# Retention attention and a mixer on one core: the order of the weight loads and of the third batch's loads in the first stretch

## The chip, the cores and the metric

The kernel runs on one core of a Trainium2 chip. The metric is the device time of one execution in microseconds (us); it is given as the median of several executions. A profile comes from one further look at a single execution, and its span is a little shorter than the time of that execution.

## The reference, cut to what matters

The inputs are q, k and v of shape (8 batches, 8 heads, 576 positions, 64), all float32, and four weight matrices. Per batch and head the kernel computes decayed causal products without a softmax, puts the heads side by side to a row of 512, and sends the result through a mixer: a low-rank product along the positions (U is 576 x 32, V is 32 x 576), a residual, and a two-layer network with relu (w1 is 512 x 2048, w2 is 2048 x 512).

```python
scores = scale * np.matmul(q, k.transpose(0, 1, 3, 2))
Dmat = np.where(rel >= 0, gamma[:, None, None] ** rel[None, :, :], 0.0)
x = np.matmul(scores * Dmat[None], v)            # then (B, S, H * D)
u = x + (x.transpose(0, 2, 1) @ U @ V).transpose(0, 2, 1)
out = u + np.maximum(u @ w_ch1, 0.0) @ w_ch2
```

## The kernel before

Two batches make a pair of 1152 rows, which is nine chunks of 128 rows; the fifth chunk (index J = 4) holds the last 64 rows of one batch and the first 64 of the next. `order` lists the chunks of all four pairs, so `order[NI]` (NI = 9) is the first chunk of the third batch. All matmuls run in bf16. The attention works chunk by chunk with a running state per head; the decay is put into the rows of q and v (or k) by the scale tables qscale, vscale and vscaleU.

The first pair is handled apart. Its two batches are cut into four units of 256 rows (units 0 and 1 of the first batch, 2 and 3 of the second) and the half chunk J. `load_u` (L625) loads a unit: k, q and v in two halves each, so six transfers of 256 KB, issued by SP. `scale_u` (L656) and `cast_u` (L648) turn them into bf16, mostly on POOL (GpSimd); `T_u` transposes them on PE; `SC_u`, `mask_u`, `RV_u`, `QS_u` and `XS_u` are scores, mask, values, the state's share and the scaling of the result (L773, on DVE); `ST_u` and `Sblk` update the state. `cast_qk` and `prep_v` (L261) do the same casts for the half chunk.

From the third batch on, a chunk is loaded with `load` (L217: k, q and v, 256 KB each, issued by SP at L230), cast by `cast_chunk` (on ACT, DVE and POOL, L280 to L291) and transposed by a DMA, `xbar` (L298, on SP). Then `section` uses it; its scores are L315.

The mixer's first layer is `Y1` (L534, PE, followed by the relu on ACT at L539), one product per block f of 128 columns of w1. The second layer is `Y2` (L568), which runs through all sixteen blocks of w2 for one chunk of 128 rows; its result is added to the residual and stored by POOL (L557, L560).

The weights come by POOL's DMA queue and are cast from float32 to bf16 on the way: `load_w1(f0, f1)` (L196) brings the columns of the blocks f0 to f1, `load_w2(f)` (L200) two blocks of w2. All of w1 comes in six pieces, all of w2 in eight.

The schedule is written out by hand: each engine executes its instructions in the order of the program text, and an instruction that waits holds everything behind it on its engine. `startup` (L884) issues the loads and prepares the first pair; `first_stretch` (L1009) handles the half chunk's second part, units 2 and 3, and fills the gaps with the first layer of the first batch (`y(n)` runs n of its sixteen blocks). After that `merge` interleaves mixer items with the sections of the next batch by cost shares: `ready(n)` casts and transposes chunk NI + n, `fetch(n, which)` loads one. SP thus issues, in this order: the loads of units 0 to 2, of unit 3, of chunks NI to NI + 2 and of k and q of chunk NI + 3, the first transpose, and further loads and transposes in turn.

Two gates hold SP's queue. `load_u` and `load` take an argument `gate`: the engine named there writes one column of the first tile of the load with a memset (L634, L223), and SP's transfer into that tile has to wait for it. In the kernel before, both unit 3 and chunk NI are gated by POOL, so these loads start when POOL comes to the memset in its own order. All staged loads use 15 buffers of one pool in turn, and a load waits until the casts of the buffer's last content are done.

POOL's order in this stretch is: the casts of the half chunk's second part, its values (`prep_v`), the w1 pieces (2, 4) and (4, 6), the scaling of unit 2's k, the casts of its q, w1 (6, 8), the memset for unit 3, the casts of unit 2's v, w1 (8, 12), the casts of unit 3's k and q, w1 (12, 16), the memset for chunk NI, the casts of unit 3's v, and the eight pieces of w2.

Of the kernel before, what the change touches and what calls it, by code (L numbers as in the profile page):

```python
# [34 lines left out]
def kernel(  # L35
# [11 lines left out]
    nc = tc.nc  # L47
# [8 lines left out]
    NF = dff // P  # L56
    NCC = dm // P
    NI = 9
# [135 lines left out]
    def load_w1(f0, f1):  # L194
        w = slice(f0 * P, f1 * P)
        nc.gpsimd.dma_start(  # L196
            out=w1_sb[:, :, w], in_=moe_w_ch1[:, w].rearrange("(c p) f -> p c f", p=P))

    def load_w2(f):
        nc.gpsimd.dma_start(  # L200
            out=w2_sb[:, f:f + 2, :],
            in_=moe_w_ch2[f * P:(f + 2) * P, :].rearrange("(f p) d -> p f d", p=P),
        )
# [10 lines left out]

    ch = {}

    def load(pr, i, which, seg=None, gate=None):  # L217
        c = ch.setdefault((pr, i), {})
        for j in which:
            if ("f", j) not in c:  # L220
                c["f", j] = stage.tile([P, H, D], FP32, tag="stage", name="stage_t")
                if gate is not None:
                    gate.memset(c["f", j][:, 0:1, 0:1], 0.0)  # L223
                    gate = None
            dram = (q, k, v)[j]
            for n_seg, (rows, b, t0) in enumerate(parts(pr, i)):
                if seg is not None and n_seg != seg:
                    continue
                n = rows.stop - rows.start
                nc.sync.dma_start(  # L230
                    out=c["f", j][rows, :, :],
                    in_=dram[b, :, t0:t0 + n, :].rearrange("h s d -> s h d"),
                )
# [27 lines left out]
    def prep_v(pr, i, rows=slice(0, P)):  # L261
        c = ch[pr, i]
        if "v" not in c:
            c["v"] = v_pool.tile([P, H, D], BF16, tag="v", name="vt")
        scale_rows(c["v"][rows], c["f", 2], i, rows, nc.gpsimd)
# [618 lines left out]
    def startup():  # L884
        load_u(0, (1, 0))
        load_v_rows()
        load_u(1, (1, 0))
        load_u(0, (2,))
        load(0, J, (1, 0), seg=0)
        load_u(1, (2,))  # L890
        load(0, J, (2,), seg=0)
        load_u_rows()
        load(0, J, (1, 0, 2), seg=1)
        load_u(2, (1, 0, 2))
        nc.gpsimd.memset(st["x", 0][HI, J, :], 0.0)

        warm(10)
        cast_unit(0)
        T_u(0, 1, nc.vector)
        un[0]["off"] = y1_tile(0)[:, 0:4, :].rearrange(  # L900
            "p (a x) (y i) -> p a (x y) i", x=2, i=P)
        nc.vector.memset(un[0]["off"][HI], 0.0)
        warm(5)
        nc.scalar.activation(out=V_b, in_=V_f, func=AF.Copy)
        T_u(0, 0, nc.scalar)
        make_v()
        warm(5)
        SC_u(0, 0, ps_sc, "psc")
        mask_u(0, 0)
        cast_unit(1)  # L910
        cast_u(0, 2, 0, nc.gpsimd)
        cast_u(0, 2, 1, nc.gpsimd)
        cast_u(1, 2, 0, nc.gpsimd)
        load_w1(0, 2)
        cast_u(1, 2, 1, nc.gpsimd)
        T_u(1, 1, nc.scalar)
        SC_u(0, 1, ps_o, "po")
        mask_u(0, 1)
        SC_off(0, ps_sc, "psc")
        warm(3)  # L920
        T_u(1, 0)
        SC_off(1, ps_o, "po")
        warm(3)
        SC_u(1, 0, ps_sc, "psc")
        mask_u(1, 0)
        cast_qk(0, J, LO, nc.scalar, nc.vector, decay=True)
        SC_u(1, 1, ps_o, "po")
        mask_u(1, 1)

        acc1 = pss_tile()  # L930
        ST_u(0, ALL, acc1, True)
        Sblk(acc1, 1)
        RV_u(0, 0)
        RV_u(0, 1)
        RV_off()
        XS_u(0)
        T_J(LO)
        acc2 = ps_big.tile([P, NHP, P], FP32, tag="big", name="pss2")
        ST_u(0, ALL, acc2, True)
        prep_v(0, J, LO)  # L940
        cast_urows()
        RV_u(1, 0)
        SC_J(LO)
        mask_J(LO)
        ST_u(1, LO, acc1, False)
        Sblk(acc1, 2)
        cast_qk(0, J, HI, nc.gpsimd, nc.gpsimd)
        prep_v(0, J, HI)
        load_w1(2, 4)
        load_w1(4, 6)  # L950
        scale_u(2, 0, nc.gpsimd)
        for hh in range(2):
            cast_u(2, 0, hh, nc.gpsimd)
        load_w1(6, 8)
        load_u(3, (1, 0, 2), nc.gpsimd)
        for hh in range(2):
            cast_u(2, 2, hh, nc.gpsimd)
        load_w1(8, 12)
        scale_u(3, 0, nc.gpsimd)
        for hh in range(2):  # L960
            cast_u(3, 0, hh, nc.gpsimd)
        load_w1(12, 16)
        load(*order[NI], (1, 0, 2), gate=nc.gpsimd)
        for hh in range(2):
            cast_u(3, 2, hh, nc.gpsimd)
        for f in range(0, NF, 2):
            load_w2(f)
        RV_u(1, 1)
        QS_u(1, 0, 1)
        XS_u(1, 0, 1)  # L970
        ST_u(1, ALL, acc2, False)
        Sblk(acc2, 3)
        QS_u(1, 1, 2)
        XS_u(1, 1, 2)
        RV_J(LO)
        QS_J(3)
        XS_J(LO)

        xT = [ps_big.tile([P, dm], FP32, tag="big", name="xT") for _ in range(3)]
        xT.append(ps_sc.tile([P, dm], FP32, tag="psc", name="xT"))  # L980

        def to_xT(lo, hi):
            for i in range(lo, hi):
                for cc in range(NCC):
                    nc.tensor.matmul(
                        xT[cc][:, i * P:(i + 1) * P],
                        st["x", 0][:, i, cc * P:(cc + 1) * P], ident,
                        start=(i == 0), stop=True, skip_group_check=True,
                    )

        to_xT(0, 2)
        MA, _, _, _ = mixer_items(0, 0, split=True)
        MA((ps_o, "po"))
        to_xT(2, J)
        for cc in range(NCC):
            g = slice(cc * R, (cc + 1) * R)
            nc.tensor.matmul(
                xT[cc], st["a", 0][g, :], V4[g, HALF:HALF + 4 * P],
                start=False, stop=True, skip_group_check=True,
            )  # L1000
        for cc in range(NCC):
            o = st["uT", 0][:, :, cc, :]
            i_ = xT[cc].rearrange("p (s t) -> p s t", t=P)
            if cc % 2 == 0:
                nc.scalar.activation(out=o, in_=i_, func=AF.Copy)
            else:
                nc.vector.tensor_copy(out=o, in_=i_)

    def first_stretch():  # L1009

        ys = iter([fn for _, fn in y1_items(0)])

        def y(n):
            for _ in range(n):
                fn = next(ys, None)
                if fn is not None:
                    fn()

        _, MH0, _, outs0 = mixer_items(0, 0, split=True)
        MA1, MH1, MT1, outs1 = mixer_items(0, 1, split=True)  # L1020
        T_J(HI)
        y(1)
        scale_u(2, 1, nc.vector)
        make_u()
        SC_J(HI)
        mask_J(HI)
        y(1)
        acc = pss_tile()
        ST_J(HI, acc)
        Sblk(acc, 0)  # L1030

        def unit(u, slots, last):
            T_u(u, 1, nc.vector)
            if last:
                y(1)
            T_u(u, 0)
            y(1)
            SC_u(u, 0, ps_sc, "psc")
            mask_u(u, 0)
            y(1)  # L1040
            ST_u(u, LO, acc, False)
            Sblk(acc, slots[1])
            SC_u(u, 1, ps_sc, "psc")
            mask_u(u, 1)
            if not last:
                scale_u(3, 1, nc.vector)
            y(1)
            if not last:
                ST_u(u, HI, acc, False)
                Sblk(acc, slots[2])  # L1050
            RV_u(u, 0)
            QS_u(u, 0, slots[0])
            QS_u(u, 1, slots[1])
            if last:
                RV_J(HI)
                XS_J(HI)
            RV_u(u, 1)
            XS_u(u)

        for g in range(NI + 1, NI + 4):  # L1060
            load(*order[g], (1, 0, 2) if g < NI + 3 else (1, 0))
        unit(2, (0, 1, 2), False)
        y(2)
        unit(3, (2, 3), True)
        y(1)
        MA1()
        y(1)
        MH1(outs1[0])
        y(2)
        MT1(outs1[0])  # L1070
        MH1(outs1[1])
        y(16)
        Y1, rest = y1_items(1, by_seg=True)
        Y1(0, 0)
        Y1(1, 0)
        MT1(outs1[1])
        MH0(outs0[0])
        Y1(2, 0)
        for f in range(3):
            Y1(f, 1)  # L1080
        return rest[3:]
# [60 lines left out]
```

## Time and profile before

| what | value |
|---|---|
| five runs | 328.24, 327.23, 330.67, 328.96, 332.22 us; median 328.96 |
| the profiled execution | 328.24 us |
| its span | 326.5 us, granted TensorE clock 1.00 |
| busy: PE, DVE, ACT, POOL | 311.6, 171.5, 143.2, 99.9 us |
| DMA queue of SP | 40.40 MB in 144512 packets |
| DMA queue of POOL | 12.32 MB in 7824 packets |
| w1 pieces issued by POOL at | 16.1, 23.0, 23.8, 27.2, 29.2, 39.4 us |
| w2 pieces issued by POOL at | 42.1 to 47.0 us (the last one's start) |
| unit 3's loads issued by SP | 28.18 to 34.8 us |
| chunk NI's loads issued by SP | from 40.32 us |
| first use of w1's second piece | 29.03 us |
| first use of w2 | 75.8 us |

PE is the matmul engine, DVE the vector engine, ACT the scalar engine, POOL is GpSimd, and SP issues DMAs. Times count from the start of the span. In the page's row of forty slices a digit is the busy share of one slice of 8.16 us in tenths. In an answer of the windows each engine has its busy time and, in brackets, its number of instructions, in the order PE, weight load, DVE, ACT, POOL; then come the granted clock, the mean busy share of the sixteen DMA engines (it can exceed 1, since both queues count) and the GB/s moved. A "landing" is the time from the issue of a DMA to the moment when its data are there.

### The profile page before, as it was taken

What the parts mean: (1) busy time and instruction counts of PE and PEld (TensorE: products, weight loads), DVE (VectorE), ACT (ScalarE), POOL (GpSimd) and SP (SyncE); (2) the same over time, 40 slices, a digit from 0 to 9 for tenths busy, and PEclk for the clock granted to TensorE, in tenths of its full rate; (3) what the DMA queues carried; (4) which work ended last, traced back from release to release, by engine and by line L of the source; (5) the groups of instructions that cost most, each with busy time, mean ns of one, the idle gap of its engine ahead of it and who ended that gap; (6) DMA issues with size and microseconds to landing.
All of it is one profiled execution on the core that took longest, in us unless ns stands there. A gap on an engine that the chain in (4) does not pass through costs nothing.

```text
span 326.5 us, 9076 instructions
## 1 busy us (share of the span) xinstructions
PE 311.6 (95%) x3860; PEld 171.2 (52%) x3885; DVE 171.5 (53%) x336; ACT 143.2 (44%) x326; POOL 99.9 (31%) x169
## 2 busy tenths in 40 slices
PE   8998899979999999999999999999999999999996
PEld 3574455745444444456744444457744444467544
DVE  7666455327745478546754477555744475510012
ACT  3747447874001285038820484048810473047400
POOL 7676470343112724132321414141421500110000
PEclk9999999999999999999999999999999999999999
DMA  7999899999984989979998599969998440340012
GB/s 207 246 228 199 206 196 196 219 208 140 248 189 118 253 179 189 211 172 165 213 156 209 132 174 221 209 152 134 206 197 198 116 68 3 97 114 0 2 73 88
DMA packets 152376, 53.30 MB, mean 163 GB/s; under 512 B 132016, under 2 KB 149808, under 8 KB 152336
## 3 DMA queue, kind: packets, MB, share of 16 engines
q1 hardware_dynamic: 144512, 40.40, 67.2%
q0 software_dynamic: 7824, 12.32, 15.5%
q8 instruction: 30, 0.49, 0.6%
q14 instruction: 10, 0.08, 0.1%
HBM read 36.85 MB, written 9.44 MB: 142 GB/s over the span
## 4 chain that ended last, share of the span: by engine, by line
PE 76%; DMA 8%; SPq 5%; ACT 3%; DVE 2%; issue 2%; POOL 2%; DVEq 0%
PE ps_y L568 36%; PE ps_y L534 32%; DMA qkT<-qk 4%; SPq L636 3%; DMA stage_t<-in_q_dram 3%; PE pp L315 2%; DMA stage_t<-in_v_dram 2%; DVE u L483 2%; SPq L230 1%; PE pp L335 1%; ACT y L539 1%; PE pp L347 1%; PE ps_y L579 1%; PE AB L377 1%; PE pa L450 1%
## 5 line engine op out<-in xcount | busy, mean ns | idle before, releaser
L534 PE MATMUL ps_y<-uT,w_sb 128*128 128x256 bf16 (+2 forms) x768 | 132.9, 326 | 1.8 <-DMA w_sb<-in_moe_w_ch_dram 0.8
L539 ACT ACTIVATE y<-ps_y 128x384 bf16<-128x384 f32 (+2 forms) x192 | 89.7, 491 | 98.7 <-PE ps_y L534 97.6
L568 PE MATMUL ps_y<-w_sb,y 128*128 128x512 bf16 x535 | 123.8, 379 | 2.2 <-issue 1.1
L534 PEld LDWEIGHTS <-w_sb 128*128 128x128 bf16 x768 | 72.2, 98 | 49.3 <-issue 2.5
L568 PEld LDWEIGHTS <-y 128*128 128x128 bf16 x560 | 52.6, 98 | 61.1
L291 POOL TENSOR_TENSOR vt<-stage_t,vscale 64x256 bf16<-64x256 f32 (+1 forms) x81 | 50.1, 619 | 71.2 <-DMA stage_t<-in_v_dram 46.0
L557 DVE TENSOR_TENSOR o_sb<-ps_y,u 128x512 f32<-128x512 f32 (+2 forms) x38 | 25.2, 664 | 81.6 <-PE ps_y L568 79.2
L560 POOL DMA_DIRECT2D out_dram<-o_sb x31 | 17.1, 553 | 104.2 <-DVE o_sb L557 98.4
L323 DVE TENSOR_TENSOR ret<-pp,triH 128x512 bf16<-128x512 f32 x27 | 18.7, 692 | 24.4 <-PE pp L347 19.0
L483 DVE TENSOR_TENSOR u<-ph,xt 128x768 bf16<-128x768 f32 (+2 forms) x24 | 21.8, 951 | 5.9 <-PE ph L477 5.9
L282 DVE CAST qk<-stage_t 64x256 bf16<-64x256 f32 x54 | 19.6, 363 | 6.8 <-DMA stage_t<-in_k_dram 5.6
L456 ACT ACTIVATE a_sb<-pa 128x128 bf16<-128x128 f32 x8 | 2.2, 278 | 43.2 <-PE pa L450 43.2
L363 DVE TENSOR_TENSOR xt<-pp,qscale 128x512 bf16<-128x512 f32 x27 | 18.6, 690 | 4.7 <-PE pp L347 4.2
L402 DVE TENSOR_TENSOR s_sb<-AB,Af 64x256 bf16<-64x256 f32 x42 | 17.7, 422 | 2.1 <-ACT s_sb L397 1.6
L357 DVE COPY q<-qkT 64x256 bf16<-64x256 bf16 x48 | 13.0, 270 | 9.7 <-DMA qkT<-qk 8.7
L283 ACT ACTIVATE qk<-stage_t 128x512 bf16<-128x512 f32 x27 | 16.8, 621 | 0.5 <-DMA stage_t<-in_q_dram 0.5
L395 ACT ACTIVATE Af<-AB 128x256 f32<-128x256 f32 x24 | 9.2, 385 | 8.1 <-PE AB L377 7.6
L654 POOL CAST qk<-stage_t 128x512 bf16<-128x512 f32 x16 | 10.2, 644 | 8.5 <-DMA stage_t<-in_q_dram 4.9
L711 DVE TENSOR_TENSOR ret<-psc,triU 128x1024 bf16<-128x1024 f32 x8 | 9.7, 1221 | 5.5 <-PE psc L703 5.5
L315 PEld LDWEIGHTS <-qkT 64*64 64x64 bf16 x432 | 5.6, 107 | 12.6 <-issue 7.8
L315 PE MATMUL pp<-qkT 64*64 64x64 bf16 x432 | 8.6, 198 | 3.1 <-DMA qkT<-qk 3.1
L280 ACT ACTIVATE qk<-stage_t 128x256 bf16<-128x256 f32 x27 | 11.0, 409 | 0.0
(123 smaller groups left out, 213.3 us busy)
## 6 DMA issues: line engine op xcount, KB each, us to landing
stage_t<-in_k_dram SPq DMA_DIRECT2D x32, 256.0 KB, 4.6
stage_t<-in_q_dram SPq DMA_DIRECT2D x32, 256.0 KB, 5.1
stage_t<-in_v_dram SPq DMA_DIRECT2D x32, 256.0 KB, 5.5
out_dram<-o_sb POOLq DMA_DIRECT2D x31, 256.0 KB, 3.5
w_sb<-in_moe_w_ch_dram POOLq DMA_DIRECT2D x12, 256.0 KB, 8.1
stage_t<-in_k_dram SPq DMA_DIRECT2D x8, 128.0 KB, 3.4
stage_t<-in_q_dram SPq DMA_DIRECT2D x8, 128.0 KB, 3.8
stage_t<-in_v_dram SPq DMA_DIRECT2D x8, 128.0 KB, 5.3
```

The costliest lines, as they stand in the source:

```text
L282: nc.vector.tensor_copy(out=o[to, hl], in_=f[fr, hl])
L291: nc.gpsimd.tensor_tensor(out=o[to, hl], in0=f[fr, hl], in1=w[fr, hl, :, None].to_broadcast([n, NHP, D]), op=ALU.mult)
L315: nc.tensor.matmul(pp[half(m), m ^ hl, hp * D:(hp + 1) * D], qkT[half(hl), NHP + hp, half(m)], qkT[half(hl), hp, half(m ^ hl)], start=True ...
L323: nc.vector.tensor_tensor(out=ret.rearrange("p a b i -> p a (b i)").rearrange("p a (b i) -> p a b i", i=D), in0=pp[:, :, 0:NHP * D].rearra ...
L363: nc.vector.tensor_tensor(out=st["x", pr][:, i, :].rearrange("p (hp hl d) -> p hl hp d", hl=2, d=D), in0=pp[:, :, NHP * D:2 * NHP * D].rea ...
L402: nc.vector.tensor_tensor(out=S_[half(x), 1, :], in0=Bk[half(1 - x)], in1=Af[half(1 - x), now, :], op=ALU.add)
L483: nc.vector.tensor_tensor(out=st["u", par][:, i0 - base:i0 - base + n, w].rearrange("p s (c d) -> p c s d", c=2), in0=ph[k][:, :, 0:n, :], ...
L534: nc.tensor.matmul(ps[:, 0:n, :], w1_sb[:, cc, f * P:(f + 1) * P], st["uT", par][:, c0:c0 + n, cc, :], start=(cc == 0), stop=(cc == NCC - 1),)
L539: nc.scalar.activation(out=st["y1", par][:, f, c0 * P:(c0 + n) * P], in_=ps[:, 0:n, :].rearrange("p s t -> p (s t)"), func=AF.Relu)
L557: nc.vector.tensor_tensor(out=o_sb[:, 0:n], in0=ps[:, 0:n], in1=st["u", par][:, c, w], op=ALU.add)
L560: (nc.sync if last else nc.gpsimd).dma_start(out=out_flat[r0:r0 + P, w], in_=o_sb[:, 0:n])
L568: nc.tensor.matmul(ps, st["y1", par][:, f, c * P:(c + 1) * P], w2_sb[:, f, :], start=(f == 0), stop=(f == NF - 1),)
```

## The change

It has four parts. The gate of `load` is taken out, and chunk NI's loads move from `startup` into the loop of `first_stretch` that already loads the following chunks (g now begins at NI). The eight `load_w2` calls move from the end of `startup` behind unit 3 in `first_stretch`, and a memset on DVE of one column of w2's first block stands in front of them; the first of these loads writes that column too, so POOL waits for DVE there. `load_w1(2, 4)` moves ahead of `prep_v(0, J, HI)`. `load_u(3, ...)` with its gate moves from behind `load_w1(6, 8)` to ahead of the casts of unit 2's q.

```diff
--- before.py
+++ after.py
@@ -214,14 +214,11 @@
 
     ch = {}
 
-    def load(pr, i, which, seg=None, gate=None):
+    def load(pr, i, which, seg=None):
         c = ch.setdefault((pr, i), {})
         for j in which:
             if ("f", j) not in c:
                 c["f", j] = stage.tile([P, H, D], FP32, tag="stage", name="stage_t")
-                if gate is not None:
-                    gate.memset(c["f", j][:, 0:1, 0:1], 0.0)
-                    gate = None
             dram = (q, k, v)[j]
             for n_seg, (rows, b, t0) in enumerate(parts(pr, i)):
                 if seg is not None and n_seg != seg:
@@ -945,14 +942,14 @@
         ST_u(1, LO, acc1, False)
         Sblk(acc1, 2)
         cast_qk(0, J, HI, nc.gpsimd, nc.gpsimd)
+        load_w1(2, 4)
         prep_v(0, J, HI)
-        load_w1(2, 4)
         load_w1(4, 6)
         scale_u(2, 0, nc.gpsimd)
+        load_u(3, (1, 0, 2), nc.gpsimd)
         for hh in range(2):
             cast_u(2, 0, hh, nc.gpsimd)
         load_w1(6, 8)
-        load_u(3, (1, 0, 2), nc.gpsimd)
         for hh in range(2):
             cast_u(2, 2, hh, nc.gpsimd)
         load_w1(8, 12)
@@ -960,11 +957,8 @@
         for hh in range(2):
             cast_u(3, 0, hh, nc.gpsimd)
         load_w1(12, 16)
-        load(*order[NI], (1, 0, 2), gate=nc.gpsimd)
         for hh in range(2):
             cast_u(3, 2, hh, nc.gpsimd)
-        for f in range(0, NF, 2):
-            load_w2(f)
         RV_u(1, 1)
         QS_u(1, 0, 1)
         XS_u(1, 0, 1)
@@ -1057,11 +1051,14 @@
             RV_u(u, 1)
             XS_u(u)
 
-        for g in range(NI + 1, NI + 4):
+        for g in range(NI, NI + 4):
             load(*order[g], (1, 0, 2) if g < NI + 3 else (1, 0))
         unit(2, (0, 1, 2), False)
         y(2)
         unit(3, (2, 3), True)
+        nc.vector.memset(w2_sb[:, 0, 0:1], 0.0)
+        for f in range(0, NF, 2):
+            load_w2(f)
         y(1)
         MA1()
         y(1)
```

## The prediction

> **What bounds the kernel now.** I read the page first, then the waits of PE, then PE's and SP's timelines between 20 and 80 us, then the windows of one microsecond where the DMA row has a hole, and last the landing times of single transfers.
>
> ```profile
> PE 311.6 (95%) x3860; PEld 171.2 (52%) x3885; DVE 171.5 (53%) x336; ACT 143.2 (44%) x326; POOL 99.9 (31%) x169
> PE   8998899979999999999999999999999999999996
> DMA  7999899999984989979998599969998440340012
> ```
>
> PE is busy 95% of the span, so only its idle time can be won. The DMA engines are full from 8 to 90 us but for a dent in the fifth slice (32.6 to 40.8; a slice is 8.16 us): the first stretch is limited by transfers as much as by PE. The waits of PE from 15 to 60 us (first three lines) and from 60 to 100 us (last) say which idle time:
>
> ```profile
> PE pst L674 <- DVE qk L658: 1.0, 1, 1.0
> PE ps_y L534 <- DMA w_sb<-in_moe_w_ch_dram: 0.8, 1, 0.8
> PE pa L450 <- DVE xt L773: 0.5, 1, 0.5
> PE pp L315 <- DMA qkT<-qk: 2.7, 2, 2.4
> ```
>
> The largest is the first scores of the third batch, which wait for the transposed keys. PE's timeline places it (start, length, in brackets the idle time before):
>
> ```profile
> 55.28 12.29 PE L534 MATMUL ps_y<-uT,w_sb 128*128 128x384 bf16 x88
> 69.98 0.32 PE L315 MATMUL pp<-qkT 64*64 64x64 bf16 x16 [2.40 <-DMA qkT<-qk]
> 75.13 0.32 PE L315 MATMUL pp<-qkT 64*64 64x64 bf16 x16 [0.26 <-DMA qkT<-qk]
> 75.77 3.63 PE L568 MATMUL ps_y<-w_sb,y 128*128 128x512 bf16 x15
> ```
>
> After 75.77 PE has no wait of note. SP's timeline shows why that transpose is late (start and issue time; long issues are SP held by a full queue):
>
> ```profile
> 40.32 0.37 SPq L230 DMA_DIRECT2D stage_t<-in_k_dram  x1
> ...
> 41.37 3.48 SPq L230 DMA_DIRECT2D stage_t<-in_v_dram  x1
> ...
> 45.88 6.76 SPq L230 DMA_DIRECT2D stage_t<-in_q_dram  x1
> ...
> 64.48 1.15 SPq L230 DMA_DIRECT2D stage_t<-in_q_dram  x1
> 65.81 1.84 SPq L298 DMA_TRANSPOSE qkT<-qk  x1
> ```
>
> The eleven chunk loads of 256 KB stand ahead of the transpose in SP's order. They start at 40.32, behind the gate (L223, on POOL at 40.18), and SP is through at 65.63. The inputs of the transpose were cast long before (ACT's q cast, L283, ends at 61.02). It lands 4.1 us after its issue, at 69.9: the bound here is transfer work. The gate's price is the hole in the DMA share (second number from the right):
>
> ```profile
> 37.00:38.00 1.00, 0.13 (x3) 0.13 (x4) 0.88 (x2) 0.39 (x1) 0.00 (x0) 1.00 1.20 316
> 38.00:39.00 1.00, 1.00 (x10) 0.61 (x9) 1.00 (x2) 0.00 (x0) 0.79 (x2) 1.00 0.79 194
> 39.00:40.00 1.00, 0.86 (x11) 0.56 (x9) 0.55 (x1) 0.72 (x2) 1.00 (x2) 1.00 0.17 46
> 40.00:41.00 1.00, 1.00 (x12) 0.34 (x15) 0.74 (x1) 0.58 (x2) 0.84 (x3) 1.00 0.35 23
> 41.00:42.00 1.00, 1.00 (x20) 0.45 (x16) 0.65 (x1) 0.59 (x1) 0.46 (x1) 1.00 0.31 47
> 42.00:43.00 1.00, 1.00 (x26) 0.70 (x24) 0.58 (x1) 0.68 (x2) 1.00 (x3) 1.00 1.26 211
> ```
>
> **The gate of the chunk loads goes.** The three gated loads follow unit 3's six in SP's order already, and no other SP instruction lies between, so the order of SP does not change, only the pause in it. Their buffers come free early: the last of the first three at 23.1 (L255 on POOL), those for the other chunks by 37.8 (L658 on DVE). The window 42 to 60 has a share of 1.23. Against it, 38 to 42 lost (4 x 1.23 - 0.79 - 0.17 - 0.35 - 0.31) / 1.23 = 2.7 us of full transfer. The memset gone from POOL is 0.12 us under a wait.
>
> **Unit 3's loads sooner.** Their memset (L634, at 28.03) now stands before two casts (1.62) and a w1 piece (0.80) and behind the scaling: about 25 us. But 20 to 28 is full (share 1.25), so it fills only the dip at 28 to 29 (0.93): (1.23 - 0.93) / 1.23 = 0.2 us. It also lets unit 3's second k piece, which landed at 28.6 + 8.4 = 37.0 and held PE 1.0 us through DVE's scaling, land sooner: by nothing at worst, by 3 us at best. I take 1.5 us, enough to remove that wait.
>
> **w1's second piece ahead of the half chunk's values.** POOL is free at 21.21 and waits 0.84 us for those values until 22.05. The issue takes 0.82 and fits there. It lands 5.9 us after its issue now (28.9); from 21.2 it is 27.1, and PE needs it at 28.2: the 0.8 us wait goes. Against this, unit 2's q and v pieces share the engines with it earlier. Unit 3's first two k pieces landed 4.5 us apart beside w1 pieces, where unit 2's came about 0.9 apart. A late q piece of unit 2 holds PE's transposes at 27.7. Between nothing and 1 us; I take 0.5. PE's own gain up to the third batch is then 0.8 + 1.0 - 0.5 = 1.3 us, with ends 0 and 1.8.
>
> **w2 behind unit 3.** The eight issues keep their place in POOL's order (behind the last cast of unit 3, ahead of the first third-batch values at 56.5); new is the wait for DVE's memset, behind XS_u(3) (L773, 46.16 to 47.39). DVE then idles 1.74 us until 49.12, which covers a memset (0.1 us, from POOL's row for the like). The issues move from 42.1 to between 45.7 and 47.5, 3.6 to 5.4 us later. Behind them POOL has nothing until the values. The last piece now lands at 47.0 + 13.7:
>
> ```profile
> L200 POOL DMA_DIRECT2D w_sb<-in_moe_w_ch_dram x2: 751/760/770, 46.3 to 47.0; - x2
> ...
> DMA to landing us min/median/max: 12.6/13.1/13.7
> ```
>
> That is 60.7; moved, 64.3 to 66.1. Its first reader is L568 at 75.8, or 72.9 by my forecast. So 7 us of slack hide it; without them each us late is a us lost. Transfer work ahead of the transpose is the same sum as before, w2 included, so the later w2 gains or costs nothing in it.
>
> A rule that speaks against this edit: the Trainium skill, "DMA: Bandwidth & Descriptors", section "Rules for kernel authors", advises issuing a DMA early and waiting on it late. By that rule taken alone the 3.6 to 5.4 us would be lost at the first reader (an estimate: 328.24 plus them, 331.8 to 333.6). The rows of landing and first use show 15 us between them today, so I do not charge it.
>
> **The sum.** Transfers: 2.7 + 0.2 = 2.9 us, so the transpose lands at 69.9 - 2.9 = 67.0. PE arrives at 67.58 - 1.3 = 66.3, so the transfer still ends last and PE's wait shrinks from 2.4 to 0.7. The second transpose hangs on the same queue and moves by the same 2.9; its 0.26 stays. After that PE has work without a hole, so 2.9 us reach the end: 328.24 (the profiled execution, span 326.5) - 2.9 = **325.3**, span 323.6. The median of the five, 328.96, lies 0.7 above the profiled one. One per cent of it is about what a measurement of this kernel tells from no change; the line is then 325.7.
>
> **Rivals.**
> (1) Every wait named above goes: PE's idle 2.40 + 0.26 + 1.0 + 0.8 = 4.5 us, 323.7. For it: with w2 later, early chunk loads may run alone. Against: the transpose must land by 65.8, 1.2 us sooner than the transfer sum allows.
> (2) The transfers' gain is given back: 0 to 2.3 us, 325.9 to 328.2. The w2 pieces crowd chunk loads (the k load issued at 44.9 beside them took 16.1 us, the one at 63.3 took 4.6), and now fall on the last chunk loads, right before the transpose. If that is worse than a shift of equal work, PE only waits longer at L315. Against: SP's loads behind w2 came every 1.2 us.
> (3) Slower: w2 arrives after its reader. The place is L568 at 72.9, the price is one us per us late; it decides from about 7 us beyond my landing, and 1% slower (332.2) needs 14 us beyond it (325.3 + 7). For: chunk loads now fill the queue before w2 starts. Against: beside the same loads w2's eight pieces landed from 48.8 to 60.7, 1.7 us apart.
>
> **How the numbers follow.** My forecast 0.52 (2.4 to 3.5 us won: 324.7 to 325.8), rival 1 0.13, rival 2 0.23, rival 3 and other losses 0.12. My own case straddles the line of 325.7, and the 0.7 between the profiled run and the median may fall on either side; I count 0.30 of it below the line and 0.22 above. Faster is 0.30 + 0.13 = 0.43; within 1% is 0.22 + 0.23 and 0.02 of small losses, 0.47; slower is the other 0.10. The range reaches from rival 1 (323.6) past rival 2 to a small loss (328.8) and leaves out the real losses.
>
> **What would show it.** The DMA share has no hole at 38 to 42; the first chunk load of the third batch is issued by 35; w2's issues start at 45 to 48 and end their landings by 67; L315's first start is near 67.0 with under 1.5 us of idle time; the waits of L674 and of the third w1 product are gone. Wrong would be: a wait of L568 for w_sb (rival 3), L315 still at 69 to 70 (rival 2) or at 66 with no wait (rival 1), or a new wait of PE for unit 2's q at 27 to 30.

## The result, and the profile after

| session | before, median (runs) | changed kernel, median (runs) | ratio, 95% interval |
|---|---|---|---|
| on record | 329.01 (80) | 326.88 (43) | 0.9963 [0.9947, 0.9979] |
| second | 329.29 (29) | 326.07 (10) | 0.9911 [0.9883, 0.9939] |
| third | 329.80 (35) | 327.94 (12) | 0.9959 [0.9931, 0.9987] |
| fourth | 330.20 (13) | 327.53 (8) | 0.9925 [0.9884, 0.9967] |

The changed kernel lies below the kernel before in every session, and every interval ends below 1. The third session alone does not show a gain, though: there the kernel before itself, run once more as if it were another kernel, came out at 0.9958, as low as the changed kernel's 0.9959. The forecast was 325.3, 2.9 us won. On record the medians differ by 2.1 us and the ratio says 1.2 us: the ratio leaves out runs over 1.5% above a kernel's fastest, and the kernel before spreads wider (325.5 to 332.7 against 324.9 to 329.8), so more of its slow runs drop out. The plain mean of the four ratios, 0.9940, is 2.0 us. That is the size to explain: the direction came out; of the amount some two thirds did by this mean, two fifths by the ratio on record.

Not all of the difference is the order of the loads. The granted TensorE clock of an execution is 0.999 or 1.000 in most, and 0.983 to 0.995 in some: in 71 of the 129 executions of the kernel before in the five sessions of the experiments, but in 5 of the 73 of the changed kernel in the table. Among executions at 0.999 or more the medians differ by 1.6, 1.5 and 1.7 us in the second to fourth session (327.68 and 326.07, 329.19 and 327.69, 328.88 and 327.18); over all executions of these sessions they differ by 3.2, 1.9 and 2.7. The prediction has no term for the clock.

The profiled execution took 326.85 us (span 325.1), 1.39 below the one of before. Lines of the changed kernel are three lower: L531 is the old L534, L565 the old L568, L312 the old L315. The page:

```profile
PE 311.2 (96%) x3860; PEld 170.9 (53%) x3885; DVE 170.5 (52%) x337; ACT 143.2 (44%) x326; POOL 99.8 (31%) x168
PE   7998899999999999999999999999999999999996
DMA  8999999998965999979998599969999340340012
```

PE's busy time is that of before (311.6) within 0.4; of the 1.4 us of span that were won, 1.0 is idle time. The dent of the fifth slice is gone from the DMA row. The waits of PE from 15 to 60 us (first three) and from 60 to 100 us (last):

```profile
PE ps_y L531 <- DMA w_sb<-in_moe_w_ch_dram: 1.6, 1, 1.6
PE pss L779 <- POOL qk L651: 0.8, 1, 0.8
PE pa L447 <- DVE w_sb L1059: 0.5, 1, 0.5
...
PE ps_y L531 <- ACT y L536: 0.6, 1, 0.6
```

The wait for unit 3's k is gone and so is the one for the transpose. Three are new: 0.8 for unit 2's v (L779), 1.6 for w1 at a later block than before, and 0.6 for a relu on ACT. PE's timeline places them:

```profile
31.52 0.38 PE L779 MATMUL pss<-qk 64*128 64x128 bf16 x4 [0.80 <-POOL qk L651]
...
40.06 1.04 PE L531 MATMUL ps_y<-uT,w_sb 128*128 128x512 bf16 x4 [1.58 <-DMA w_sb<-in_moe_w_ch_dram]
...
67.66 0.32 PE L312 MATMUL pp<-qkT 64*64 64x64 bf16 x16
...
70.60 2.77 PE L531 MATMUL ps_y<-uT,w_sb 128*128 128x256 bf16 x20 [0.65 <-ACT y L536]
73.30 0.32 PE L312 MATMUL pp<-qkT 64*64 64x64 bf16 x16
...
73.93 3.63 PE L565 MATMUL ps_y<-w_sb,y 128*128 128x512 bf16 x15
```

L312 starts at 67.66 with no idle time: here PE came last and not the transpose. POOL's timeline says where the 1.6 comes from (start, busy, idle before):

```profile
26.86 0.80 POOL L196 DMA_DIRECT2D w_sb<-in_moe_w_ch_dram  x1
29.30 0.61 POOL L651 CAST qk<-stage_t 128x512 bf16<-128x512 f32 x1 [1.64 <-DMA stage_t<-in_v_dram]
30.86 0.61 POOL L651 CAST qk<-stage_t 128x512 bf16<-128x512 f32 x1 [0.95 <-DMA stage_t<-in_v_dram]
31.41 0.74 POOL L196 DMA_DIRECT2D w_sb<-in_moe_w_ch_dram  x1
```

In the kernel before, the same stretch of POOL reads:

```profile
27.23 0.80 POOL L196 DMA_DIRECT2D w_sb<-in_moe_w_ch_dram  x1
28.03 0.12 POOL L634 MEMSET stage_t<- 128x1 f32 x1
28.07 1.17 POOL L654 CAST qk<-stage_t 128x512 bf16<-128x512 f32 x2
29.18 0.74 POOL L196 DMA_DIRECT2D w_sb<-in_moe_w_ch_dram  x1
```

POOL now waits 1.64 and 0.95 us for unit 2's v, for which it did not wait at all before. The issue behind those casts, w1's fifth piece (blocks 8 to 11), goes out at 31.41 in place of 29.18, and PE's ninth block waits for it. And the DMA share, in windows of two microseconds from 40 on (second number from the right):

```profile
40.00:42.00 2.00, 1.94 (x23) 0.88 (x24) 0.50 (x1) 0.60 (x1) 0.10 (x1) 1.00 1.23 214
42.00:44.00 2.00, 2.00 (x30) 1.01 (x28) 1.36 (x2) 1.35 (x3) 0.00 (x0) 1.00 1.02 215
44.00:46.00 2.00, 2.00 (x51) 1.46 (x50) 1.01 (x2) 0.60 (x1) 0.00 (x0) 1.00 0.54 123
46.00:48.00 2.00, 1.55 (x25) 0.65 (x24) 1.51 (x3) 0.68 (x2) 0.15 (x1) 1.00 0.99 223
```

The hole at 38 to 42 is closed, and another has opened at 42 to 48, while w2 waits for unit 3. SP's and POOL's timelines of the same stretch, a line of each:

```profile
40.83 3.65 SPq L227 DMA_DIRECT2D stage_t<-in_q_dram  x1
```

```profile
47.85 5.62 POOL L200 DMA_DIRECT2D w_sb<-in_moe_w_ch_dram  x8 [7.75 <-DVE w_sb L1059]
```

SP is held for 3.65 us with the issue of a chunk load, although the share falls meanwhile, and w2 comes only at 47.85. Why SP is held there while the share falls the views do not show. That a long issue means a full queue is my reading of rows like those of the kernel before, where with no load under way two issues take 0.37 and 0.53 us and the third 3.48; how full the queue is stands in no view.

The last loads ahead of the first transpose, the casts of its inputs on ACT, and the transpose:

```profile
51.06 7.01 SPq L227 DMA_DIRECT2D stage_t<-in_q_dram  x1
60.55 0.62 ACT L280 ACTIVATE qk<-stage_t 128x512 bf16<-128x512 f32 x1
61.19 4.14 SPq L295 DMA_TRANSPOSE qkT<-qk  x1
```

SP is through with the loads at 58.07 (before: 65.63) and then waits for ACT, whose cast ends at 61.17: the transpose is issued 4.6 us sooner than before (65.81). But it lands 6.2 us after its issue, at 67.4, where it took 4.1 before (69.9). In all eleven profiles with w2 behind unit 3 this landing takes 5.6 to 7.8 us, in all nine with w2 at its old place 3.8 to 4.5: w2's pieces, of which the last lands at 65.1, now move beside the transpose.

### The profile page after: what moved, and what is told of

Same layout as the page of the kernel before. It is cut to its first block, busy times and chain, and to the rows that moved or that the text cites. A ratio compares the mean times of both kernels' runs of the same rounds, so it can differ in the third digit from the quotient of the medians.

```text
span 325.1 us, 9087 instructions
## 1 busy us (share of the span) xinstructions
PE 311.2 (96%) x3860; PEld 170.9 (53%) x3885; DVE 170.5 (52%) x337; ACT 143.2 (44%) x326; POOL 99.8 (31%) x168
## 4 chain that ended last, share of the span: by engine, by line
PE 75%; ACT 4%; DMA 3%; DVE 2%; issue 1%; DVEq 0%
PE ps_y L565 34%; PE ps_y L531 32%; PE pp L312 2%; DVE u L480 2%; DMA uT<-u 1%; ACT y L536 1%; DMA qkT<-qk 1%; PE pp L332 1%; PE pp L344 1%; PE ps_y L576 1%; PE AB L374 1%; PE pa L447 1%; PE ph L474 1%; ACT s_sb L389 1%; ACT qk L280 0%
## 5 line engine op out<-in xcount | busy, mean ns | idle before, releaser
L531 PE MATMUL ps_y<-uT,w_sb 128*128 128x256 bf16 (+2 forms) x768 | 133.1, 326 | 4.0 <-DMA w_sb<-in_moe_w_ch_dram 1.6
L565 PE MATMUL ps_y<-w_sb,y 128*128 128x512 bf16 x535 | 123.8, 379 | 2.2 <-issue 1.1
L531 PEld LDWEIGHTS <-w_sb 128*128 128x128 bf16 x768 | 72.2, 98 | 51.9 <-issue 3.7
L565 PEld LDWEIGHTS <-y 128*128 128x128 bf16 x560 | 52.6, 98 | 61.1
L354 DVE COPY q<-qkT 64x256 bf16<-64x256 bf16 x48 | 13.1, 273 | 13.1 <-DMA qkT<-qk 12.2
L279 DVE CAST qk<-stage_t 64x256 bf16<-64x256 f32 x54 | 18.6, 344 | 1.2
L280 ACT ACTIVATE qk<-stage_t 128x512 bf16<-128x512 f32 x27 | 16.8, 623 | 0.7 <-DMA stage_t<-in_q_dram 0.6
L277 ACT ACTIVATE qk<-stage_t 128x256 bf16<-128x256 f32 x27 | 11.1, 410 | 0.0
L312 PEld LDWEIGHTS <-qkT 64*64 64x64 bf16 x432 | 5.6, 107 | 9.6 <-issue 8.2
L191 PE MATMUL pw<-ident 128*128 128x512 bf16 x26 | 8.5, 476 | 1.4 <-POOL ident masks.py:199 1.4
```

The costliest lines, as they stand in the source:

```text
L279: nc.vector.tensor_copy(out=o[to, hl], in_=f[fr, hl])
L280: nc.scalar.activation(out=c["qk"][:, 0, :], in_=c["f", 0].rearrange("p h d -> p (h d)"), func=AF.Copy)
L531: nc.tensor.matmul(ps[:, 0:n, :], w1_sb[:, cc, f * P:(f + 1) * P], st["uT", par][:, c0:c0 + n, cc, :], start=(cc == 0), stop=(cc == NCC - 1),)
L565: nc.tensor.matmul(ps, st["y1", par][:, f, c * P:(c + 1) * P], w2_sb[:, f, :], start=(f == 0), stop=(f == NF - 1),)
```

## The experiments

PE's first product with w1 starts anywhere from 24.0 to 25.3 us in the profiles below, so I read each profile by stretches and not by the time from its start: A from PE's first product with w1 to the long row of 88 products (L534 or L531, 12.29 us in every profile), B on to the first scores of the third batch, C on to the first product with w2, D to the end of the span. All are differences of starts in PE's timeline. The last column is the DMA time lost between 38 and 48 us: the sum over two-microsecond windows of (1.23 - share) x 2 / 1.23, where the share is lower.

| kernel | A | B | A+B | C | D | lost 38 to 48 |
|---|---|---|---|---|---|---|
| before | 30.78 | 14.70 | 45.48 | 5.79 | 250.73 | 2.7 |
| before, again | 32.20 | 13.65 | 45.85 | 6.02 | 250.87 | 2.7 |
| changed | 31.42 | 12.23 | 43.65 | 6.27 | 251.17 | 1.9 |
| changed, second | 29.68 | 12.25 | 41.93 | 6.23 | 250.63 | 1.5 |
| changed, third | 30.81 | 13.37 | 44.18 | 6.58 | 250.68 | 2.0 |
| changed, fourth | 30.63 | 13.62 | 44.25 | 5.98 | 250.77 | 2.1 |
| only later half | 35.14 | 12.61 | 47.75 | 5.94 | 250.70 | 1.3 |
| only later half, again | 30.80 | 13.40 | 44.20 | 6.11 | 250.79 | 0.9 |
| only early half | 31.97 | 12.22 | 44.19 | 6.27 | 251.45 | 1.4 |
| only early half, again | 32.33 | 13.41 | 45.74 | 5.94 | 250.70 | 1.0 |
| changed, w2 at old place | 30.10 | 12.22 | 42.32 | 6.27 | 250.66 | 0.4 |

B is 12.2 in the profiles where PE does not wait for the transpose: that is PE's own work, and what is above it is almost all waiting for the transpose. D lies between 250.6 and 251.5 whatever the kernel, and its mean is 250.8 for the kernel before and for the changed one: what is won on the mean lies before the first product with w2. In two of the profiles, the second of before and the first of only the later half, A holds some 3.4 us at half the granted clock (see the kernel before once more, below).

**Halves of the change (first session; before 329.50, 35 runs).** Theory A: the gate and w2 carry the gain, and the early half gives nothing, as its new waits eat the old ones. Theory B: the early half carries it.

Only the later half (w1's second piece and unit 3's loads back at their old places):

```diff
-        load_w1(2, 4)
         prep_v(0, J, HI)
+        load_w1(2, 4)
...
         scale_u(2, 0, nc.gpsimd)
-        load_u(3, (1, 0, 2), nc.gpsimd)
...
         load_w1(6, 8)
+        load_u(3, (1, 0, 2), nc.gpsimd)
```

> The gate of the third batch's chunks is out and w2 is behind unit 3, but w1's second piece and unit 3's loads keep their old places. Theory A (this half carries the gain, the early half gives nothing): PE waits 0.8 for w1's second piece and 1.0 for unit 3's k as before, and no 1.6 for w1's fifth piece; the first transpose of the third batch lands at 67 to 68, PE starts it there; time equal to the changed kernel within 0.5 us or up to 1 us better, ratio to before 0.992 to 0.998. Theory B (the early half carries it): L315's line starts at 69 or later, ratio 0.998 to 1.002.

Measured: 327.88 median, ratio 0.9988 [0.9955, 1.0022]. Its profile was its slowest execution; A alone is 35.1 there, as PE waits 1.81 us for a cast on POOL and the granted clock is 0.50 from about 42.5 to 46 us behind that wait. L312 starts at 72.06, not at the 67 to 68 that was expected.

Only the early half, in the kernel before:

```diff
+        load_w1(2, 4)
         prep_v(0, J, HI)
-        load_w1(2, 4)
...
         scale_u(2, 0, nc.gpsimd)
+        load_u(3, (1, 0, 2), nc.gpsimd)
...
         load_w1(6, 8)
-        load_u(3, (1, 0, 2), nc.gpsimd)
```

> Only w1's second piece and unit 3's loads move; the gate and w2's place stay as before. Theory A: the waits for w1's second piece and unit 3's k go, new ones for unit 2's v (0.8) and w1's fifth piece (1.6) come, and the chunk loads start when the gate falls, about 37 to 39 in place of 40; the transpose lands at 68 to 70; ratio 0.997 to 1.002. Theory B: ratio 0.995 or below.

Measured: 327.08, ratio 0.9941 [0.9910, 0.9972]. The waits came as theory A said (0.9 for unit 2's v, 1.2 for w1's fifth piece), and the kernel was faster all the same. That speaks against theory A, which allowed 0.997 at best. The gate's memset falls at 38.74.

Only the gate taken out, w2 and the early order as before:

```diff
-        load(*order[NI], (1, 0, 2), gate=nc.gpsimd)
...
-        for g in range(NI + 1, NI + 4):
+        for g in range(NI, NI + 4):
```

> Only the gate goes; w2 is issued at its old place (about 42), the early order is the old one. If the transfers ahead of the first transpose are one sum of work whatever their order, it lands at 67 to 67.6 as in the changed kernel, and the ratio is that of e1_late_only within 0.002 (w2's later place gives nothing). If w2's later place is what helps (w2's pieces crowd the chunk loads), it lands at 69 or later and the ratio is 0.998 to 1.002.

Measured: 328.06, ratio 0.9954 [0.9924, 0.9984]. In its profile A is 32.62 and B 13.13, and the transpose landed at 70.1, not at 67 to 67.6: of the two expectations the landing fits the second and the ratio the first. By the medians the kernel stands with the later half (327.88): w2's later place adds nothing that shows.

The changed kernel with w1's fifth piece ahead of the casts that held it:

```diff
         load_w1(6, 8)
+        load_w1(8, 12)
         for hh in range(2):
             cast_u(2, 2, hh, nc.gpsimd)
-        load_w1(8, 12)
```

> The changed kernel with w1's fifth piece (blocks 8 to 11) issued ahead of the casts of unit 2's v, so that it no longer waits on POOL behind their landing (issue at about 27.7 in place of 31.4). If that place is the cause of the new 1.6 us wait at PE's ninth block, the wait is gone and PE comes to the third batch 1.0 to 1.6 us sooner (66.1 to 66.7 on the changed kernel's clock), where the first transpose (67.3) then ends last: 0.3 to 0.5 us won, ratio to before 0.993 to 0.996. If the piece is late because its transfer is slowed by unit 3's loads and not because of its issue, the wait stays above 1 us. A late unit 2 v (wait of 0.8 now) may grow to 1.5.

Measured: 327.53, ratio 0.9952 [0.9927, 0.9976]; the changed kernel did not run beside it. The wait of 1.6 is gone, so the place of the issue was its cause. Its waits from 15 to 60 us (first two) and from 60 to 100 us (last):

```profile
PE pst L671 <- POOL qk L651: 0.9, 1, 0.9
PE pss L779 <- POOL qk L651: 0.6, 1, 0.6
...
PE pp L312 <- DMA qkT<-qk: 1.6, 2, 1.3
```

Unit 3's q is late instead (0.9), and what PE won it then waits for at the transpose (1.3). Here a piece that goes first made another late.

**What limits the changed kernel (second session; before 329.29, 29 runs).** Theory D: early transfers land up to 2 us sooner or later, and the gate hands this on.

> The changed kernel once more, as the measure for the three kernels beside it and as a second profile of it. Half edits alone (only the early half 0.994, only the later half 0.999, only the gate out 0.995, all to before) came out near the whole change, so the parts do not add. Theory D: the early transfers land up to 2 us sooner or later from one execution to the next, and the gate hands this to the third batch's loads in the kernel before; without a gate on that path it does not. Then this profile shows other early waits than the first one (sum of PE's waits from 15 to 60 us anywhere from 2 to 5 us), and the ratio is 0.992 to 0.997.

The changed kernel again: 326.07. Its profile has a wait of 0.8 for w1's fifth piece and none for unit 2's v, the transpose lands as PE arrives (66.0), and the span is 322.8.

w2 at its old place in POOL's order, all else as changed:

```diff
             cast_u(3, 2, hh, nc.gpsimd)
+        for f in range(0, NF, 2):
+            load_w2(f)
...
-        nc.vector.memset(w2_sb[:, 0, 0:1], 0.0)
-        for f in range(0, NF, 2):
-            load_w2(f)
```

> The changed kernel with w2 issued at its old place in POOL's order (about 40 us) and no memset on DVE; the gate stays out, the early half stays in. In the changed kernel the DMA share falls again between 42 and 48 us, as w2 waits for unit 3. If transfers ahead of the first transpose were the limit, filling this hole lands the transpose up to 1.5 us sooner. If PE is the limit there (it started L312 without a wait), the time stays: ratio within 0.002 of the changed kernel beside it. If w2's pieces crowd the chunk loads, the transpose lands at 68.5 or later, PE waits 1 us or more and the time is 0.5 to 1.5 us worse.

Measured: 325.88 against 326.07 beside it, no difference. The windows of its profile, 42 to 48:

```profile
42.00:44.00 2.00, 2.00 (x34) 1.08 (x34) 1.36 (x2) 1.35 (x3) 2.00 (x4) 1.00 1.03 207
44.00:46.00 2.00, 2.00 (x51) 1.52 (x52) 1.00 (x2) 0.60 (x1) 2.00 (x4) 1.00 1.21 217
46.00:48.00 2.00, 1.55 (x26) 0.65 (x25) 1.22 (x1) 0.87 (x2) 1.86 (x4) 1.00 1.24 203
```

The hole is filled (0.54 in the changed kernel at 44 to 46, 1.21 here). L312 had no wait in either profile, and the 0.65 for ACT stays. Filling the hole won nothing here, where PE and not the transpose came last.

The last two kernels' edits that moved transfers, together (the diffs of w2 at its old place and of w1's fifth piece ahead of unit 2's v casts):

> As the kernel with w2 at its old place, and w1's fifth piece ahead of the casts of unit 2's v. That edit alone took PE's 1.6 us wait away and left a 1.3 us wait for the transpose in its place. If both limits are lifted together, PE comes to L312 at about 66.5 and waits less than 0.7: 0.5 to 1.2 us better than the changed kernel. If the transpose does not land before 68, nothing is won.

Measured: 326.99, 0.9 above the changed kernel beside it: a miss. PE waits 1.0 for unit 2's v and 1.0 for unit 3's q, and the hole at 38 to 42 is back (1.7 of the 2.0 us lost between 38 and 48): w1's last piece stands behind the casts of unit 3's q on POOL, which wait for it until 38.89, and is issued at 39.45, w2 from 41.36.

The third chunk's casts one item later, so that ACT has the relu first:

```diff
-(0.20, ready(2))
+(0.235, ready(2))
```

> The changed kernel with the third batch's third chunk cast one item later in the merge (ready(2) at 0.235 in place of 0.20), so that ACT's two casts of it (0.93 us) come behind the first relu of the pair that PE waits 0.65 us for at about 70. If that order on ACT is why the stall came back, the wait is gone and 0.4 to 0.65 us are won (ratio 0.998 to 0.9987 to the changed kernel beside it). If PE waits for ACT's work as a whole, the wait only moves by one block and the time is the same.

Measured: 326.56 against 326.07. The stall on ACT went from 0.65 to 0.2 in the profile, but no time was won; here PE came early and waited 0.35 for the transpose.

**The early half's two parts (third session; before 329.80, 35 runs).**

> The changed kernel a third time, as the measure for the kernels beside it. Its first two profiles differ by 2.3 us of span: the second has no wait for unit 2's v and half the wait for w1's fifth piece (0.8 in place of 1.6). If that is the play of transfers from one execution to the next, the third lies between them: span 322.5 to 325.5, first start of L312 at 65.5 to 68, ratio 0.990 to 0.997.

The changed kernel: 327.94, span 326.5 and L312 at 69.24, each a microsecond above the upper end of what was expected. The transpose ended last (L312 waits 1.1 twice).

w1's second piece back at its place, unit 3's loads sooner:

```diff
-        load_w1(2, 4)
         prep_v(0, J, HI)
+        load_w1(2, 4)
```

> The changed kernel with w1's second piece back behind the half chunk's values; unit 3's loads stay sooner. If moving that piece is what makes unit 2's v and, behind its casts on POOL, w1's fifth piece late, those waits (0 to 0.8 and 0.8 to 1.6) shrink, a wait of about 0.8 for the second piece comes back, and the time is the changed kernel's within 0.5 us. If the piece's move carries part of the gain, it is 0.5 to 1.0 us slower.

Measured: 327.90, the same. The wait for that piece is back (1.2), the one for the fifth piece shrinks (0.4), unit 2's v makes none: by these profiles the piece's move trades one wait for two others.

Unit 3's loads back, w1's second piece ahead:

```diff
         scale_u(2, 0, nc.gpsimd)
-        load_u(3, (1, 0, 2), nc.gpsimd)
...
         load_w1(6, 8)
+        load_u(3, (1, 0, 2), nc.gpsimd)
```

> The changed kernel with unit 3's loads back behind w1's fourth piece; w1's second piece stays ahead. If unit 3's earlier loads carry the early half's gain, PE waits 1 us or more for unit 3's k or q at its transposes again, L312 starts 1 to 2 us later than in the changed kernel beside it, and the time is 1 to 2 us more, near that of the kernel with only the later half (1.6 us below before by medians). If they carry nothing, the time is the changed kernel's within 0.5 us.

Measured: 327.38, ratio 0.9958 [0.9928, 0.9988], not the 1 to 2 us above the changed kernel beside it that unit 3's loads would have been worth; its profile, its slowest execution, has A+B of 45.65. With the gate out, the early place of these loads shows no gain.

The kernel before once more:

> The kernel before once more, for a second profile of it. Theory D: the gate falls when unit 3's q has been cast, and what that varies by is handed on. Then the gate's memset, the first transpose's landing and L315's first start move together against the first profile (40.2, 69.9 and 70.0), by up to 2 us either way, and the hole in the DMA share lies right ahead of the memset again. If the transpose does not follow the gate, theory D falls.

Measured over 8 runs: 328.24, ratio to the same kernel's other runs 0.9958 [0.9916, 1.0000], so a ratio of one session is good to some 0.4%. Gate at 39.92, transpose landed at 70.0, L315 at 70.01, hole ahead of the memset as before. Nothing of these moved by more than 0.3, so this run neither shows theory D nor excludes it. What did move is the clock. PE waits 1.81 us for w1's second piece (0.82 in the first profile), and behind that wait the granted clock is 0.50 for some 3.4 us (third number from the right):

```profile
28.00:29.00 1.00, 0.00 (x0) 0.00 (x0) 0.79 (x2) 0.60 (x1) 0.35 (x1) 1.00 1.40 188
29.00:30.00 1.00, 0.32 (x1) 0.11 (x2) 0.00 (x0) 0.00 (x0) 0.77 (x2) 0.90 1.32 184
30.00:31.00 1.00, 1.00 (x4) 0.30 (x2) 0.00 (x0) 0.00 (x0) 0.52 (x1) 0.50 1.35 246
31.00:32.00 1.00, 1.00 (x19) 0.41 (x17) 0.00 (x0) 0.48 (x1) 0.00 (x0) 0.50 1.18 310
32.00:33.00 1.00, 1.00 (x7) 0.42 (x4) 0.89 (x1) 0.12 (x1) 0.00 (x0) 0.50 1.16 316
33.00:34.00 1.00, 1.00 (x11) 0.45 (x8) 0.34 (x1) 0.34 (x1) 0.54 (x1) 0.89 1.07 206
```

From that product to the next row of eight, PE takes 7.41 us (29.68 to 37.09) for the work that took 5.82 in the first profile (29.03 to 34.85). L315 starts no later for it, as PE waits less for the transpose (1.36 in place of 2.40).

**All three candidates for the missing part (fourth session; before 330.20, 13 runs).**

> The changed kernel once more, as the measure beside the next three; medians so far 1.9 to 3.2 us below before. Mean 326 to 328, ratio 0.991 to 0.997.

The changed kernel: 327.53. L312 waits 1.3 for the transpose.

w1's fifth piece split, so that the ninth block needs half of it:

```diff
-        load_w1(8, 12)
+        load_w1(8, 10)
+        load_w1(10, 12)
```

> The changed kernel with w1's fifth piece (blocks 8 to 11, 512 KB) issued as two of two blocks each, one behind the other; the bytes are the same. PE's ninth block needs only the first. If the 0.4 to 1.6 us wait there is for the whole piece, it falls below 0.5 and PE comes to L312 about 0.8 us sooner; as the first transpose lands near the same time (0.4 after PE to 1.1 before it), the time falls by 0 to 0.5 us. If PE were the limit alone, it would fall by 0.8 or more. POOL has one issue more (0.8 us).

Measured: 326.93. The wait at the ninth block is gone and A is 29.21; B is 13.42, so the transpose ends last again.

w2 at its old place and ACT's casts later (both diffs as in the second session):

> The changed kernel with w2 at its old place in POOL's order, which filled the hole at 42 to 48 and left L312 without a wait, and with the third chunk's casts one item later, which took 0.45 of ACT's 0.65 us stall away. Each alone gave no time that could be told from the changed kernel. If the stall on ACT is what is left on the path once the transpose is early, the two together win 0.4 to 0.7 us; if ACT's work is late as a whole, nothing.

Measured: 326.74. Neither a hole nor a wait at L312; C is 5.83.

All three (the two of the kernel above and the split):

> Both of these edits and the split of w1's fifth piece together: PE's early wait, the hole in the transfers and ACT's order are all taken at once. If the three are what kept the forecast's 2.9 us from coming out whole, this one is 0.7 to 1.3 us faster than the changed kernel beside it (ratio 0.988 to 0.992 where that one is at 0.992 to 0.996). If the rest of the gap is the play of the first 20 us, which no edit here touches, it is within 0.4 us of it.

Measured: 326.50, ratio 0.9898 [0.9861, 0.9934], the lowest median of its session, 1.0 below the changed kernel by medians. The split alone (326.93) and the pair above (326.74) give nearly as much, and with 6 to 8 runs of each the intervals overlap: the kernel lies below both others here, but not by a margin that is clear of noise against the changed one.

**The halves once more (fifth session; before 329.69, 17 runs).** The two kernels of the first session, unchanged.

> Only the later half (gate out, w2 behind unit 3) once more, as its first profile was its slowest execution (330.4 of 327.0 to 330.4). If the gate's place in the queue carries the gain, as the forecast had it, the stretch from PE's first w1 product to the first scores of the third batch is 43.5 to 44.5 us here, near the changed kernel's mean of 43.5, and the ratio is at or below the early half's beside it. If the early place of unit 3's loads carries it, the stretch is 45 us or more, as in the other three profiles with these loads at their old place (45.5 to 45.9), and the time is 0.5 to 1.5 us above the early half's.

> Only the early half (w1's second piece and unit 3's loads sooner; gate and w2 as before) once more. If unit 3's loads carry the gain, the stretch is 43 to 44.5 us again (44.2 in the first profile) and the ratio 0.992 to 0.996. If the first result was the draw, the stretch is 45 or more and the ratio above 0.996.

Measured: only the later half 327.73, ratio 0.9950 [0.9915, 0.9986], A+B 44.20; only the early half 325.68, ratio 0.9891 [0.9835, 0.9947], A+B 45.74 in a profile that was the slowest of its six runs. The windows of the early half:

```profile
38.00:40.00 2.00, 1.82 (x21) 1.17 (x18) 0.84 (x2) 1.19 (x3) 0.88 (x3) 1.00 0.65 66
40.00:42.00 2.00, 0.74 (x4) 0.31 (x4) 0.58 (x1) 0.64 (x2) 1.83 (x3) 1.00 1.19 197
```

With the gate still in, the hole is down to 1.0 us (1.4 in the first profile, 2.7 before): the gate's memset falls at 38.22, since the casts ahead of it find unit 3's q sooner.

By the medians the later half alone wins 1.6 and 2.0 us, the early half alone 2.4 and 4.0, the whole 1.9 to 3.2. The parts do not add, and the early half alone is no worse than the whole. Neither of the two expectations came out whole: A+B of the later half fits the gate as the carrier, but its ratio is above the early half's; the early half's ratio fits unit 3's loads, but its A+B does not. Single profiles do not decide here which part carries the gain.

## Why the prediction was wrong in its size

**What bounds the kernel** was read rightly as far as the stretch goes: the gain lies ahead of the first product with w2, and the mean of D is the same (250.8). That transfer work alone bounds the first transpose did not last: in the changed kernel its issue (61.19) follows the end of ACT's cast (61.17), as it does within 0.03 us in the second and fourth profile, and its landing takes longer.

**The gate's hole, "2.7 us of full transfer".** This is the step that failed. The 2.7 was measured rightly (2.7 again in the second profile of before), but the change does not close it: over the four profiles the changed kernel still loses 1.9 us between 38 and 48, only later, as w2 no longer comes to fill the time. Where w2 is back at its old place, the loss is 0.4. The gate's removal was credited with the whole, so the hole shrank by 0.8 and not by 2.7. Nor is a microsecond of hole a microsecond of landing, as the sum has it: with w2 early and the hole nearly gone (0.4, 0.3 and 0.0 us lost in three kernels) the transpose landed at 66.5, 67.8 and 68.2, against a mean of 67.9 in the changed kernel. The later place of w2 lets SP's loads end sooner and makes the transpose itself slower, and the two about cancel. How much of the missing time each of these makes is not shown.

**Unit 3's loads, "only the dip at 28 to 29", 0.2 us.** Mis-sized in the other direction. The gate stood behind unit 3's q casts on POOL, so sooner loads pull the gate itself forward and close 1.3 to 1.7 us of the same hole. The two parts were priced as if each had its own stretch; they share one, which fits the halves not adding, and so does the kernel with the gate out and these loads back at their old place, which lost nothing.

**PE's own gain, 1.3 us (ends 0 and 1.8).** A is 31.5 on the mean of the two profiles before and 30.6 on the mean of the four after: 0.85, with single values from -0.6 to +1.1 against the first profile of before. Some 1.6 us of the second profile's 32.2 are its half clock, so against the first profile alone the mean gain is 0.15. I bounded the late q piece of unit 2 and left out its v, and with it what stands behind v's casts on POOL: w1's fifth piece, 0.8 to 1.6 us at PE's ninth block.

**The transpose, 2.9 us sooner.** It landed at 67.4, 65.9, 69.2 and 69.0, a mean of 67.9, 2.0 us sooner than the 69.9 before; A+B went from 45.7 to 43.5, 2.2 us. In two of four profiles the transfer ended last, as forecast; in the other two PE and the transpose met.

**"After that PE has work without a hole".** Wrong by 0.4: C rose from 5.9 to 6.3 on the mean. In the two profiles where PE does not stall at the transpose it runs into ACT, which casts the third chunk (0.93 us, L277 and L280) ahead of the relu that PE waits for. With these casts one item later and w2 early, C is 5.83 where it was 6.27. In the third profile it is the second transpose (1.05 us) that makes C long.

The sum in place of mine: 0.85 in A, 1.3 in B, less 0.4 in C, 1.8 us; the mean ratio says 2.0. Of A and B only the sum is firm, as the half clock in the second profile of before makes A longer and B shorter.

**w2 and its reader.** Nearly as forecast: the issues start at 47.85, 5.75 us later than before (3.6 to 5.4 forecast). The last pieces land 11.5 and 12.4 us after their issues, the last at 52.7 + 12.4 = 65.1 (forecast 64.3 to 66.1), and L565 reads at 73.93, 8.8 us later; no profile has a wait of L565 for w2. The Trainium skill, "DMA: Bandwidth & Descriptors", section "Rules for kernel authors", advises to issue a DMA early and to wait for it late; by that advice taken alone the prediction had put a loss of 3.6 to 5.4 us (an estimate). No run shows such a loss, with the reader 9 us behind the landing, and with w2 early again the time was the same (325.88 against 326.07).

**The rivals.** The third (w2 after its reader) did not come. The first (all waits gone) is near the changed kernel's best profile: L312 at 65.94 with no wait, span 322.8. The second (L315 still at 69 to 70) is what two of the four profiles show, 69.24 and 69.05: w2's pieces did not crowd the last loads, which end 2 to 10 us sooner, but the transpose behind them, and other waits took the place of the one removed. The forecast's own sign, near 67.0 with under 1.5 us of idle time, is in one (67.66).

**What stays open.** Why one session gives 3.2 us and another 1.9; what makes the clock fall in over half of the executions of the kernel before, and how much of its wider spread that is (the second profile holds such a fall, and the transpose's wait covered it there); whether theory D has a share in it; whether the early half alone is better than the whole (0.9941 and 0.9891 against 0.9911 to 0.9963, overlapping, on different sessions); and why SP stays held while the DMA share falls at 42 to 46.

## What to carry to other kernels

When two edits remove waits that hang on the same queue, price them on the same stretch: ask what would be left for the second if the first were already in. For a load that moves ahead of others, follow the engine that waits for the overtaken one and look at what is issued behind that wait, not only at who reads the data. Take two profiles of the kernel before where transfers fill the first stretch; one that lies a microsecond off decides a forecast of three. And look at the granted clock of the single executions before a sum is made from the profile of one at full clock.

## What the runs showed that I had not expected

Removing a gate did not keep the DMA engines busy: with eleven chunk loads in SP's order the share still fell to 0.54, 0.43 and 0.35 at 44 to 46 us in three profiles, around the end of single issues of 3.6 to 3.7 us that held SP until 44.5 to 45.3 (7.01 beside w2). Only the second queue's transfers filled it (1.21 with w2 at its old place).

The granted clock falls in some executions and not in others of the same kernel. In the 71 executions of the kernel before that have 0.995 or less the median is 330.01 us, in the other 58 it is 328.57; for the changed kernel 329.34 (5 executions) and 326.85 (68). In the two profiles that hold a fall, it begins within about 0.4 us of the end of a PE wait of 1.81 us and lasts some 3.4 us at 0.50. The length of the wait alone does not decide it: waits of 1.94 and 2.40 us in other profiles left the clock at 1.00.

The same kernel, run as another for one session, came out at 0.9958 [0.9916, 1.0000] of itself.
